# Attention with forget gates and a feed-forward network on one core: a tile of turned blocks per pair, split writes, product with v at the end of its slot, one tile of rounded q

## The chip, the cores and the metric

One core of a Trainium2 chip runs the whole program. The metric is the device time of one execution in microseconds. Engine names: PE is TensorE, DVE is VectorE, ACT is ScalarE, POOL is GpSimd, SP is the engine that issues the DMAs.

## The reference

64 heads (8 batches of 8 heads) of causal attention with 576 tokens and 64 columns per head, whose scores get a decay from the running sum of the logarithms of f. The heads of a batch are joined to 512 columns, and a layer norm with a two-layer network and a residual follows.

```python
scores = scale * q @ k.T                      # scale = 1/8, per batch and head
cum = np.cumsum(np.log(np.clip(f, 1e-4, 1.0)), axis=-1)
scores = np.where(causal, -1e9, scores + cum[:, :, :, None] - cum[:, :, None, :])
attn = softmax(scores)                        # sum + 1e-9 in the denominator
x = (attn @ v) -> (8, 576, 512)
xn = (x - mean) / sqrt(var + 1e-6) * g_ln
out = x + np.maximum(xn @ w_ch1, 0) @ w_ch2   # 512 -> 2048 -> 512
```

All is float32. The weights reach the device as 64-bit floats.

## The kernel before

Products that must keep float32 accuracy are made from rounded parts: a number is split into a high part (rounded, type fp32r) and a low part (the rest), and TensorE multiplies high by high, high by low and low by high.

The attention is cut in 256 slots: for each of 64 heads the row blocks t = 1 to 4 (128 queries each, with 192, 320, 448 and 576 keys; a block t=0 of 64 queries is done along with t=1). Heads 0 to 15 are "full": their products are in plain float32, and p is turned by TensorE. Heads 16 to 63 take another way, and most of the change concerns them:

- Q: the scores (qk_mm), two products for each piece of a row block. The first reads the high parts `hi`, the second reads `xq` (a copy of the rounded q beside two rows of ones) and `kl` (the low part of k beside the gates' sums).
- S: VectorE adds the mask and finds the row's extreme (softmax_a, L425). e: ScalarE's exponential with the row sum (L436). B: VectorE adds 1e-9 and inverts (L441, L442), and POOL scales p (L443).
- T: in the next slot VectorE turns p in blocks of 32 by 32 into the tile `pb` (turn, L461 and L463). The blocks are put in their final order by way of DRAM: `write` stores `pb` to `pd` (L471), and two slots after t=2 or t=4 V reads `pd` back into `pt` (L482, four DMAs). Blocks t=0, 1, 2 make pair 2, blocks t=3, 4 make pair 4.
- H and G: four slots after t=2 or t=4 ScalarE rounds `pt` into `ph` (L498 the rows and columns needed first, L502 the rest). l: VectorE writes the low part of the first columns (L506). o: POOL writes the low part of the rest (L513).
- A: five slots after, TensorE multiplies with v (av_unit, L606): high parts first, then low parts. F: ScalarE copies half of the result (L647). a: VectorE adds the other half into `xs` (L658), and every second head stores `xs` to DRAM (L660).

The feed-forward network works on 18 chunks of 256 tokens with 16 steps each. One step goes into each slot from slot 35 on, as soon as the heads of a batch are done; the steps that are left follow after the last slot. M is a step's first product (mm1, L691 to L693), r its Relu on ScalarE (L699), m its low part on VectorE (L704), N the second product of the step before (mm2, L713 to L715), R fetches and splits the next chunk's x (L674, L676) and turns rows back (chunk_rows), b copies these (L754) and takes their mean and variance.

Other letters: k rounds the next head's k and q and makes their low parts (t=1 and t=3), x copies the rounded q into `xq` (L353), P rounds v (L362), D loads raw q and k and v, W, w, f, g and s decode the weights during the first heads, L makes reciprocal roots.

The order of work on every engine is written by hand. For each slot the letters of one string are gone through from left to right, and each emits its instructions; each engine takes its own in that order. The string in force depends on the slot number:

```python
ORDERS = [
    (0, "WwQsSthAeMrgFBmlLNPaRf"),
    (37, "WwkQSTstAMhPeHlgNFGrxfmBoVDLRba"),
    (66, "kQSTAHeVGFtlahBoMPrxmNbRLD"),
]
```

PSUM is handed out by `bank`, six banks in turn for scores, products, first layers and turned rows; a bank is reused when its reader six allocations before is done.

Of the kernel before, what the change touches and what calls it, by code (L numbers as in the profile page):

```python
# [8 lines left out]
F32 = mybir.dt.float32  # L9
# [8 lines left out]
P = 128  # L18
# [40 lines left out]
def attn_moe(ctx: ExitStack, tc: tile.TileContext, qk, v, f, g, w1, w2, out):  # L59
# [26 lines left out]
    def busy(n):  # L86
# [6 lines left out]
    mask = const.tile([P, S], F32, tag="mask", name="mask")  # L93
    nc.gpsimd.memset(mask, 0.0)
    nc.gpsimd.affine_select(
        out=mask[:, S - P :], in_=mask[:, S - P :], pattern=[[-1, P]], base=0,
# [207 lines left out]
    def new_xq(name, dt):  # L304
        xq = work.tile([66, S], dt, tag="xq", bufs=2, name=name)
        nc.gpsimd.memset(xq[64:66, :].bitcast(F32), 1.0)
        return xq

    def load(n):
        h = Head()  # L310
        h.n, h.full = n, n < NFULL
        if h.full:
            h.kl = work.tile([66, S], F32, tag="kl", bufs=2, name=f"kl{n}")
            if len(xfs) < 2:
                xfs.append(new_xq(f"xf{n}", F32))
# [36 lines left out]
    def queries_copy(h):  # L352
        nc.scalar.copy(out=h.xq[0:64, :], in_=h.hi[0:64, 0, :].bitcast(F32))  # L353
# [36 lines left out]
    corners, padded, turned = [], {}, []  # L390
# [16 lines left out]
    def row_tile(h, t):  # L407
        nm = f"p{h.n}_{t}"
        if h.full and (4 * h.n + t - 1) % 3 == 0:
            if "late" in pools:  # L410
                return pools["late"].tile([P, 4 * 9 * 32], F32, tag="pb", bufs=1, name=nm)[:, 0:S]
            return wpool.tile([P, S], F32, tag="p", bufs=1, name=nm)
        return work.tile([P, S], F32, tag="p", bufs=2, name=nm)

    def softmax_a(h, t):
        q0, m, w = QT[t]
        nm = f"{h.n}_{t}"
        if t == 0:
            pt = corner(h.n)
        else:  # L420
            pt = row_tile(h, t)
        st = work.tile([P, 4], F32, tag="st", bufs=6, name=f"st{nm}")
        off = S - P - (w - m)
        for i, (a, z, sp) in enumerate(h.s[t]):
            nc.vector.tensor_tensor_reduce(  # L425
                out=pt[:m, a:z], in0=sp, in1=mask[:m, off + a : off + z], scale=-SCALE,
                scalar=3.0e38 if i == 0 else st[:m, 0:1], op0=ALU.add, op1=ALU.min, accum_out=st[:m, i : i + 1],
            )
        h.p = getattr(h, "p", {})
        h.p[t] = (pt, st)  # L430
# [16 lines left out]
    SLOTS = {0: (0, 0), 1: (1, 3), 2: (2, 4), 3: (0, 2), 4: (1, 5)}  # L447
# [5 lines left out]
    def turn(h, t):  # L453
        if not turned:
            turned.append(pools["late"].tile([P, 4 * 9 * 32], F32, tag="pb", bufs=1, name="pb"))
            nc.gpsimd.memset(turned[0], 0.0)
        pt, out_ = h.p[t][0], blocks(turned[0], t)
        first, rest = SLOTS[t]
        m = QT[t][1]
        rows = slice(64, P) if t == 0 else slice(0, P)  # L460
        nc.vector.transpose(out_[rows, 0:2, first, :], pt[:m, 0:64].rearrange("p (b i) -> p b i", i=32))  # L461
        if t > 0:
            nc.vector.transpose(  # L463
                out_[:, :, rest : rest + t, :].rearrange("p b k i -> p k b i"),
                pt[:, 64 : 64 + P * t].rearrange("p (k b i) -> p k b i", b=4, i=32),
            )

    def write(h, t):
        w = (6 if t == 2 else 9) * 32
        pd = dram.tile([P, 4 * w], F32, tag=f"pd{t}", bufs=2, name=f"pd{t}_{h.n}")  # L470
        nc.sync.dma_start(out=pd, in_=turned[0][:, : 4 * w])  # L471
        h.pd = getattr(h, "pd", {})
        h.pd[t] = pd

    def read(h, t):
        w, z = (6 * 32, 3 * 32) if t == 2 else (9 * 32, 2 * 32)
        tag = "pt1" if t == 2 else "pt2"
        pt = pools["late"].tile([P, 4 * w], F32R, tag=tag, bufs=1, name=f"{tag}_{h.n}")
        src = h.pd[t].rearrange("(a j) (b r) -> b j a r", a=4, b=4)
        for b in range(4):  # L480
            r = z if b > 1 else 0
            nc.sync.dma_start(  # L482
                out=pt[32 * b : 32 * b + 32, :].bitcast(F32).rearrange("j (a r) -> j a r", a=4)[:, :, r:],
                in_=src[b][:, :, r:],
            )
        h.pt = getattr(h, "pt", {})
        h.pt[t] = pt

    def parts_of(h, t):
        z = 3 if t == 2 else 2  # L490
        return z, blocks(h.pt[t], t), blocks(h.ph[t], t)

    def high_first(h, t):
        tag, w = ("ph1", 768) if t == 2 else ("ph2", 9 * P)
        h.ph = getattr(h, "ph", {})
        h.ph[t] = work.tile([P, w], F32R, tag=tag, bufs=1, name=f"{tag}_{h.n}")
        z, pt, ph = parts_of(h, t)
        nc.scalar.copy(out=ph[0:64, :, 0:z, :], in_=pt[0:64, :, 0:z, :].bitcast(F32))  # L498

    def high_rest(h, t):  # L500
        z, pt, ph = parts_of(h, t)
        nc.scalar.copy(out=ph[:, :, z:, :], in_=pt[:, :, z:, :].bitcast(F32))  # L502

    def low_first(h, t):
        z, pt, ph = parts_of(h, t)
        nc.vector.tensor_tensor(  # L506
            out=ph[64:128, :, 0:z, :], in0=pt[0:64, :, 0:z, :].bitcast(F32), in1=ph[0:64, :, 0:z, :].bitcast(F32),
            op=ALU.subtract,
        )

    def low_rest(h, t):
        z, pt, ph = parts_of(h, t)
        nc.gpsimd.tensor_tensor(  # L513
            out=pt[:, :, z:, :], in0=pt[:, :, z:, :].bitcast(F32), in1=ph[:, :, z:, :].bitcast(F32), op=ALU.subtract
        )
# [54 lines left out]
    def av_unit(h, t):  # L570
# [26 lines left out]
        z, low, high = parts_of(h, t)  # L597

        def acc(c0, c1, k, r, first=False):
            n = (c1 - c0) // P  # L600

            def view(x):
                return x[:, :, r : r + 3 * n - 2 : 3, :] if t == 4 and 1 <= k <= 3 else x[:, :, r : r + n, :]
# [7 lines left out]
            one(po[:, c0:c1], vv[:, k].rearrange("p a d -> p (a d)"), high, first)  # L611
# [4 lines left out]
        if t == 2:  # L616
            acc(0, 384, 0, 0, True)
            acc(128, 384, 1, 3)
            acc(256, 384, 2, 5)
            h.o = (po[:, 64:384], S1, 0)  # L620
        else:
            acc(0, 256, 0, 0, True)
            for k in range(1, 4):
                acc(0, 256, k, 1 + k)
# [26 lines left out]
    def finish_add(h):  # L651
# [210 lines left out]
    slots += [None] * (DONE + 1)  # L862
# [15 lines left out]
    for u, slot in enumerate(slots):  # L878
# [18 lines left out]
        def piece(c):  # L897
# [16 lines left out]
            elif c == "T" and past is not None:  # L914
                for i in [1, 0] if past[1] == 1 else [past[1]]:
                    turn(hd[past[0]], i)
                if past[1] in (2, 4):
                    write(hd[past[0]], past[1])
            elif c == "V" and due_read is not None:
                read(hd[due_read[0]], due_read[1])  # L920
            elif c == "H" and late is not None:
                high_first(hd[late[0]], late[1])
            elif c == "G" and late is not None:
                high_rest(hd[late[0]], late[1])
            elif c == "l" and late is not None:
                low_first(hd[late[0]], late[1])
            elif c == "k":
                two = before(2)
                if two is not None and two[1] == 4 and not hd[two[0]].full:
                    values_low(hd[two[0]])  # L930
# [3 lines left out]
            elif c == "x" and slot is not None and n + 1 >= NFULL and n + 1 < B * H and t == 3:  # L934
# [11 lines left out]
            elif c == "e" and slot is not None:  # L946
                for i in tiles(h, t):
                    softmax_e(h, i)
            elif c in FILL:
# [5 lines left out]
            elif c == "F" and av is not None:  # L955
                finish(av)
            elif c == "a" and av is not None:
                finish_add(av)
# [50 lines left out]
        def prep():  # L1009

            if before(1) is not None and before(1)[1] == 4 and not hd[before(1)[0]].full:
                values_high(hd[before(1)[0]])
# [56 lines left out]
```

## Time and profile before

| what | value |
|---|---|
| median of 3 runs | 1288.72 us (1286.53 to 1291.04) |
| the profiled execution | 1285.22 us, its span 1283.2 us |
| mean granted clock of TensorE | 0.987 |
| PE, DVE, ACT, POOL busy | 90%, 60%, 50%, 46% |
| DMA | 186.91 MB, 165169 packets |

The span is the time from the first to the last instruction that the profile holds. Busy shares are means over stages: slots of full heads (to about 283 us, with the weights decoded beside them), slots of the other heads (to about 1053 us), and the feed-forward steps that are left. "Idle before" a group of instructions is time in which its engine had nothing to run, with what ended it. PEld are weight loads, which run beside the products.

### The profile page before, as it was taken

Reading aid. Unit: us, or ns where it says so; the run is one execution under the profiler, and the core shown is the slowest. Engines: PE = TensorE matmul, PEld = TensorE weight load, DVE = VectorE, ACT = ScalarE, POOL = GpSimd, SP = SyncE. Lnnn points to the kernel's source line nnn. Section 1 sums busy time; section 2 is a strip of 40 time slices with the busy share of each in tenths; the row PEclk is TensorE's granted clock in tenths of the full one; section 3 lists DMA queues with packets and bytes.
Section 4 is the critical chain, followed back from the end, with each engine's and each line's share of the span. In section 5 each row is a group of like instructions: output and inputs, shape, how many; then the busy total and the mean of one; then the engine's idle time right before and its main releaser. Section 6 shows DMA issues by size and latency. Waiting matters only on the chain. (4 is left out here: it accounts for less than half of the span.)

```text
span 1283.2 us, 24610 instructions
## 1 busy us (share of the span) xinstructions
PE 1159.3 (90%) x7648; PEld 1025.9 (80%) x7648; DVE 770.7 (60%) x2706; ACT 646.2 (50%) x1744; POOL 594.3 (46%) x870
## 2 busy tenths in 40 slices
PE   8889999888988888988888988889888889999998
PEld 6657888778887787878787878788787879999997
DVE  6777774576757576666667676766666672222222
ACT  6886665455555555545555555555455542111111
POOL 3454454465556565555655565655555541000000
PEclk9999999999999999999999999999999999999999
DMA  6555532656656555647565656556565642110100
GB/s 182 161 146 159 159 83 66 187 165 184 185 169 178 161 172 186 195 153 203 174 182 175 200 166 179 157 186 180 170 189 175 187 149 60 45 38 18 50 25 25
DMA packets 165169, 186.91 MB, mean 146 GB/s; under 512 B 45488, under 2 KB 131504, under 8 KB 165040
## 3 DMA queue, kind: packets, MB, share of 16 engines
q1 hardware_dynamic: 165040, 185.35, 48.5%
q8 instruction: 61, 1.00, 0.3%
q14 instruction: 68, 0.56, 0.2%
HBM read 118.93 MB, written 66.36 MB: 144 GB/s over the span
## 5 line engine op out<-in xcount | busy, mean ns | idle before, releaser
L443 POOL TENSOR_SCALAR p<-p,st 64x64 f32<-64x64 f32 (+4 forms) x320 | 169.6, 535 | 434.6 <-DVE st L442 196.7
L691 PE MATMUL h<-x,w1h 128*128 128x256 f32 x1152 | 336.0, 292 | 0.4 <-DVE st L425 0.4
L692 PE MATMUL h<-x,w1h 128*128 128x256 f32 x1152 | 328.8, 285 | 0.0
L693 PE MATMUL h<-x,w1l 128*128 128x256 f32 x1152 | 328.8, 285 | 0.0
L436 ACT ACTIVATE p<-p,st 64x64 f32<-64x64 f32 (+4 forms) x320 | 179.1, 560 | 264.4 <-DVE st L425 244.9
L704 DVE SCALAR_TENSOR_TENSOR hh<-h,hh 128x256 fp32r<-128x256 f32 x288 | 121.7, 422 | 229.1 <-ACT hh L699 227.5
L713 PE MATMUL acc<-w2h,hh 128*128 128x512 f32 x576 | 230.7, 401 | 0.0
L714 PE MATMUL acc<-w2l,hh 128*128 128x512 f32 x576 | 229.8, 399 | 0.0
L699 ACT ACTIVATE hh<-h 128x256 fp32r<-128x256 f32 x288 | 109.6, 380 | 237.7 <-PE h L693 236.1
L715 PE MATMUL acc<-w2h,hh 128*128 128x512 f32 x576 | 227.0, 394 | 0.0
L691 PEld LDWEIGHTS h<-x,w1h 128*128 128x128 f32 x1152 | 221.6, 192 | 5.5 <-issue 0.9
L692 PEld LDWEIGHTS h<-x,w1h 128*128 128x128 f32 x1152 | 222.9, 193 | 2.5
L693 PEld LDWEIGHTS h<-x,w1l 128*128 128x128 f32 x1152 | 223.1, 194 | 0.0
L425 DVE CUSTOM_DVE_ANT_0 p<-s,mask 64x64 f32<-64x64 f32 (+4 forms) x320 | 130.5, 422 | 82.4 <-PE s L385 76.6
L513 POOL TENSOR_TENSOR pt<-pt,ph 128x384 fp32r<-128x384 f32 x96 | 149.5, 1558 | 6.1 <-ACT ph L502 6.1
L606 PE MATMUL o<-pt,vv 128*64 128x256 f32 (+1 forms) x288 | 48.9, 278 | 101.4 <-POOL pt L513 97.8
L715 PEld LDWEIGHTS acc<-w2h,hh 128*128 128x128 f32 x576 | 109.7, 190 | 25.3
L713 PEld LDWEIGHTS acc<-w2h,hh 128*128 128x128 f32 x576 | 111.3, 193 | 14.5 <-ACT ph_full L568 0.2
L606 PEld LDWEIGHTS o<-pt,vv 128*64 128x64 f32 x288 | 29.6, 135 | 115.4 <-POOL pt L513 115.4
L714 PEld LDWEIGHTS acc<-w2l,hh 128*128 128x128 f32 x576 | 111.0, 193 | 12.0
L658 DVE TENSOR_TENSOR xs<-o,ot 64x320 f32<-64x320 f32 x96 | 43.2, 450 | 125.8 <-ACT ot L647 125.8
L776 POOL TENSOR_SCALAR sv<-sv 128x2 f32<-128x2 f32 x18 | 3.9, 215 | 188.9 <-DVE sv L760 187.7
(87 smaller groups left out, 2013.9 us busy)
## 6 DMA issues: line engine op xcount, KB each, us to landing
raw<-in_qk_dram SPq DMA_DIRECT2D x96, 288.0 KB
pd<-pb SPq DMA_DIRECT2D x48, 576.0 KB
pd<-pb SPq DMA_DIRECT2D x48, 384.0 KB
wr<-in_w_dram SPq DMA_DIRECT2D x32, 512.0 KB
pt<-pd SPq DMA_DIRECT2D x96, 144.0 KB
pt<-pd SPq DMA_DIRECT2D x96, 112.0 KB
vr<-in_v_dram SPq DMA_DIRECT2D x64, 160.0 KB
out_dram<-xt SPq DMA_DIRECT2D x36, 256.0 KB
```

The lines of the kernel that those rows point to most:

```text
L425: nc.vector.tensor_tensor_reduce(out=pt[:m, a:z], in0=sp, in1=mask[:m, off + a : off + z], scale=-SCALE, scalar=3.0e38 if i == 0 else st[: ...
L436: nc.scalar.activation(pt[:m, :w], pt[:m, :w], AF.Exp, bias=st[:m, i : i + 1], scale=-1.0, accum_out=st[:m, 2:3])
L443: nc.gpsimd.tensor_scalar(out=pt[:m, :w], in0=pt[:m, :w], scalar1=st[:m, 3:4], scalar2=1.0, op0=ALU.mult, op1=ALU.mult)
L513: nc.gpsimd.tensor_tensor(out=pt[:, :, z:, :], in0=pt[:, :, z:, :].bitcast(F32), in1=ph[:, :, z:, :].bitcast(F32), op=ALU.subtract)
L691: mm(ph, w1h[:, k, fs], c.x[k][:, 0, :], start=(k == 0), stop=False)
L692: mm(ph, w1h[:, k, fs], c.x[k][:, 1, :], start=False, stop=False)
L693: mm(ph, w1l[:, k, fs], c.x[k][:, 0, :], start=False, stop=(k == KT - 1))
L699: nc.scalar.activation(h[:, 0, :], c.ph, AF.Relu)
L704: nc.vector.scalar_tensor_tensor(out=h[:, 1, :], in0=ph, scalar=0.0, in1=h[:, 0, :].bitcast(F32), op0=ALU.max, op1=ALU.subtract)
L713: mm(c.acc[i], h[:, 0, ts_], w2h[:, j, :], start=(j == 0), stop=False)
L714: mm(c.acc[i], h[:, 0, ts_], w2l[:, j, :], start=False, stop=False)
L715: mm(c.acc[i], h[:, 1, ts_], w2h[:, j, :], start=False, stop=(j == FT - 1))
```

## The change

For heads 16 to 63:

- Each pair has a tile of turned blocks of its own (`pb2`, `pb4`), and the blocks lie in another order (`SLOTS`). Each t from 1 to 4 writes its own columns (`WRITES`; t=0 goes with t=1) by itself, at the end of its turn's slot (letter d), so a head has four writes for two.
- The reads take all rows and columns.
- The exponential and the softmax's second part follow directly on the turn; the cast of `pt` is one instruction and comes behind them, and the two low parts behind it. POOL's low part is two instructions.
- The product with v stands behind both feed-forward products of its slot. The copy of its result, the sum and the store come one slot later (`fin`), the store at that slot's end (letter X).
- `xq` is one tile for two, and its copy moves from t=3 to t=4. The rounding of v and its low part come one slot later.
- The mask tile has 128 columns fewer, and the feed-forward's limit and the empty slots at the end move by one slot.

```diff
 ORDERS = [
-    (0, "WwQsSthAeMrgFBmlLNPaRf"),
-    (37, "WwkQSTstAMhPeHlgNFGrxfmBoVDLRba"),
-    (66, "kQSTAHeVGFtlahBoMPrxmNbRLD"),
+    (0, "WwQsSthAeMrgFBmlLNPaXRf"),
+    (37, "WwkQSTstAMhPeHlgNFrxfmBoDLRbaXdV"),
+    (67, "kQSTeBHloFaMNAPxrmbRLdDVX"),
 ]
...
-        if len(xqs) < 2:
-            xqs.append(new_xq(f"xq{len(xqs)}", F32R))
-        h.xq = xqs[(n - NFULL) % 2]
...
     def queries_copy(h):
+        if not xqs:
+            xqs.append(new_xq("xq", F32R, work))
+        h.xq = xqs[0]
         nc.scalar.copy(out=h.xq[0:64, :], in_=h.hi[0:64, 0, :].bitcast(F32))
...
-    SLOTS = {0: (0, 0), 1: (1, 3), 2: (2, 4), 3: (0, 2), 4: (1, 5)}
+    SLOTS = {0: (1, 0), 1: (2, 0), 2: (3, 4), 3: (3, 0), 4: (4, 5)}
+    WRITES = {1: (0, 3), 2: (3, 6), 3: (0, 4), 4: (4, 9)}
...
     def write(h, t):
+        i = t + t % 2
+        w = (6 if i == 2 else 9) * 32
+        h.pd = getattr(h, "pd", {})
+        if t % 2 == 1:
+            h.pd[i] = dram.tile([P, 4 * w], F32, tag=f"pd{i}", bufs=2, name=f"pd{i}_{h.n}")
+        r0, r1 = WRITES[t]
+        a, b = (x.rearrange("p (b r) -> p b r", b=4)[:, :, 32 * r0 : 32 * r1] for x in (h.pd[i], turned[i]))
+        nc.sync.dma_start(out=a, in_=b)
...
+    FIRSTS = {2: (1, 4), 4: (3, 5)}
...
-    def high_first(h, t):
+    def high(h, t):
...
+        nc.scalar.copy(out=h.ph[t], in_=h.pt[t].bitcast(F32))
...
     def low_rest(h, t):
+        pt, ph = parts_of(h, t)
+        w = 6 if t == 2 else 9
+        for r in (slice(0, FIRSTS[t][0]), slice(FIRSTS[t][1], w)):
+            nc.gpsimd.tensor_tensor(
+                out=pt[:, :, r, :], in0=pt[:, :, r, :].bitcast(F32), in1=ph[:, :, r, :].bitcast(F32), op=ALU.subtract
+            )
...
         if j == 1:
-            nc.sync.dma_start(out=(xd1 if g1 else xd2)[b][P * pr : P * pr + P, :], in_=xs)
+            h.store = ((xd1 if g1 else xd2)[b][P * pr : P * pr + P, :], xs)
...
+        fin = av if av is not None and av.full else None
+        if before(DONE + 1) is not None and before(DONE + 1)[1] in (2, 4) and not hd[before(DONE + 1)[0]].full:
+            fin = hd[before(DONE + 1)[0]]
...
+            elif c == "d" and past is not None:
+                write(hd[past[0]], past[1])
...
-            elif c == "x" and slot is not None and n + 1 >= NFULL and n + 1 < B * H and t == 3:
+            elif c == "x" and slot is not None and n + 1 >= NFULL and n + 1 < B * H and t == 4:
                 queries_copy(hd[n + 1])
...
-                moe.limit = min(NCHUNK, max(0, min(u - LAG - 1, max(4 * NFULL, u - DONE))) // (4 * H) * S // C)
+                moe.limit = min(NCHUNK, max(0, min(u - LAG - 1, max(4 * NFULL, u - DONE - 1))) // (4 * H) * S // C)
```

More of the change, by code (lines that the diff above doesn't have):

```diff
@@ L92, in attn_moe @@
     busy(WARM[1])
-    mask = const.tile([P, S], F32, tag="mask", name="mask")
+    mask = const.tile([P, S - P], F32, tag="mask", name="mask")
     nc.gpsimd.memset(mask, 0.0)
     nc.gpsimd.affine_select(
-        out=mask[:, S - P :], in_=mask[:, S - P :], pattern=[[-1, P]], base=0,
+        out=mask[:, S - 2 * P :], in_=mask[:, S - 2 * P :], pattern=[[-1, P]], base=0,
         channel_multiplier=1, compare_op=ALU.is_ge, fill=NEG,
@@ L302, in attn_moe, with new_xq @@
     xqs, xfs = [], []
-    def new_xq(name, dt):
-        xq = work.tile([66, S], dt, tag="xq", bufs=2, name=name)
+    def new_xq(name, dt, pool):
+        xq = pool.tile([66, S], dt, tag="xq", bufs=1, name=name)
         nc.gpsimd.memset(xq[64:66, :].bitcast(F32), 1.0)
@@ L388, in qk_mm @@
             h.s[t].append((a, z, sp))
-    corners, padded, turned = [], {}, []
+    corners, padded, turned = [], {}, {}
     def padded_keys(tag, width, zeros):
@@ L410, in row_tile @@
             if "late" in pools:
-                return pools["late"].tile([P, 4 * 9 * 32], F32, tag="pb", bufs=1, name=nm)[:, 0:S]
+                return pools["late"].tile([P, 4 * 9 * 32], F32, tag="pb4", bufs=1, name=nm)[:, 0:S]
             return wpool.tile([P, S], F32, tag="p", bufs=1, name=nm)
@@ L422, in softmax_a @@
         st = work.tile([P, 4], F32, tag="st", bufs=6, name=f"st{nm}")
-        off = S - P - (w - m)
+        off = S - 2 * P - (w - m)
         for i, (a, z, sp) in enumerate(h.s[t]):
             nc.vector.tensor_tensor_reduce(
-                out=pt[:m, a:z], in0=sp, in1=mask[:m, off + a : off + z], scale=-SCALE,
+                out=pt[:m, a:z], in0=sp, in1=mask[:m, max(0, off + a) : max(0, off + a) + z - a], scale=-SCALE,
                 scalar=3.0e38 if i == 0 else st[:m, 0:1], op0=ALU.add, op1=ALU.min, accum_out=st[:m, i : i + 1],
@@ L454, in turn @@
         if not turned:
-            turned.append(pools["late"].tile([P, 4 * 9 * 32], F32, tag="pb", bufs=1, name="pb"))
-            nc.gpsimd.memset(turned[0], 0.0)
-        pt, out_ = h.p[t][0], blocks(turned[0], t)
+            for i, w in ((2, 6), (4, 9)):
+                turned[i] = pools["late"].tile([P, 4 * w * 32], F32, tag=f"pb{i}", bufs=1, name=f"pb{i}")
+                nc.gpsimd.memset(turned[i], 0.0)
+        pt, out_ = h.p[t][0], blocks(turned[t + t % 2 if t > 0 else 2], t)
         first, rest = SLOTS[t]
@@ L468, in write, with read @@
     def write(h, t):
-        w = (6 if t == 2 else 9) * 32
[L470 to L476, printed above, removed]
+        i = t + t % 2
[6 more added lines that the diff above has]
+        nc.sync.dma_start(out=a, in_=b)
+    def read(h, t):
+        w = (6 if t == 2 else 9) * 32
         tag = "pt1" if t == 2 else "pt2"
@@ L480, in read @@
         for b in range(4):
-            r = z if b > 1 else 0
             nc.sync.dma_start(
-                out=pt[32 * b : 32 * b + 32, :].bitcast(F32).rearrange("j (a r) -> j a r", a=4)[:, :, r:],
-                in_=src[b][:, :, r:],
+                out=pt[32 * b : 32 * b + 32, :].bitcast(F32).rearrange("j (a r) -> j a r", a=4), in_=src[b]
             )
@@ L487, in read @@
         h.pt[t] = pt
+    FIRSTS = {2: (1, 4), 4: (3, 5)}
     def parts_of(h, t):
-        z = 3 if t == 2 else 2
-        return z, blocks(h.pt[t], t), blocks(h.ph[t], t)
-    def high_first(h, t):
+        return blocks(h.pt[t], t), blocks(h.ph[t], t)
+    def high(h, t):
         tag, w = ("ph1", 768) if t == 2 else ("ph2", 9 * P)
@@ L496, in high_first @@
         h.ph[t] = work.tile([P, w], F32R, tag=tag, bufs=1, name=f"{tag}_{h.n}")
[L497 to L502, printed above, removed]
+        nc.scalar.copy(out=h.ph[t], in_=h.pt[t].bitcast(F32))
     def low_first(h, t):
-        z, pt, ph = parts_of(h, t)
+        pt, ph = parts_of(h, t)
+        r = slice(*FIRSTS[t])
         nc.vector.tensor_tensor(
-            out=ph[64:128, :, 0:z, :], in0=pt[0:64, :, 0:z, :].bitcast(F32), in1=ph[0:64, :, 0:z, :].bitcast(F32),
+            out=ph[64:128, :, r, :], in0=pt[0:64, :, r, :].bitcast(F32), in1=ph[0:64, :, r, :].bitcast(F32),
             op=ALU.subtract,
@@ L511, in low_rest @@
     def low_rest(h, t):
[L512 to L515, printed above, removed]
+        pt, ph = parts_of(h, t)
+        w = 6 if t == 2 else 9
[3 more added lines that the diff above has]
+            )
     def tr(out_, in_):
@@ L596, in av_unit, with acc @@
         vv = h.vv
-        z, low, high = parts_of(h, t)
-        def acc(c0, c1, k, r, first=False):
+        low, high_ = parts_of(h, t)
+        def acc(c0, c1, k, r, step=1, first=False):
             n = (c1 - c0) // P
             def view(x):
-                return x[:, :, r : r + 3 * n - 2 : 3, :] if t == 4 and 1 <= k <= 3 else x[:, :, r : r + n, :]
+                return x[:, :, r : r + step * (n - 1) + 1 : step, :]
             def one(o, st, x, first):
@@ L609, in one @@
                 )
-            one(po[:, c0:c1], vv[:, k].rearrange("p a d -> p (a d)"), high, first)
+            one(po[:, c0:c1], vv[:, k].rearrange("p a d -> p (a d)"), high_, first)
             if k > 0:
@@ L616, in av_unit @@
         if t == 2:
-            acc(0, 384, 0, 0, True)
-            acc(128, 384, 1, 3)
+            acc(0, 384, 0, 1, first=True)
+            acc(128, 384, 1, 0, 4)
             acc(256, 384, 2, 5)
@@ L621, in av_unit @@
         else:
-            acc(0, 256, 0, 0, True)
+            acc(0, 256, 0, 3, first=True)
             for k in range(1, 4):
-                acc(0, 256, k, 1 + k)
+                acc(0, 256, k, k - 1, 5)
             acc(128, 256, 4, 8)
@@ L659, in finish_add, with store @@
         if j == 1:
-            nc.sync.dma_start(out=(xd1 if g1 else xd2)[b][P * pr : P * pr + P, :], in_=xs)
+            h.store = ((xd1 if g1 else xd2)[b][P * pr : P * pr + P, :], xs)
+    def store(h):
+        if getattr(h, "store", None) is not None:
+            out_, xs = h.store
+            nc.sync.dma_start(out=out_, in_=xs)
+            h.store = None
     class Chunk:
@@ L861, in attn_moe @@
     nu = len(slots)
-    slots += [None] * (DONE + 1)
+    slots += [None] * (DONE + 2)
     hd = {}
@@ L921, in piece @@
             elif c == "H" and late is not None:
-                high_first(hd[late[0]], late[1])
-            elif c == "G" and late is not None:
-                high_rest(hd[late[0]], late[1])
+                high(hd[late[0]], late[1])
             elif c == "l" and late is not None:
@@ L927, in piece @@
             elif c == "k":
-                two = before(2)
-                if two is not None and two[1] == 4 and not hd[two[0]].full:
-                    values_low(hd[two[0]])
+                three = before(3)
+                if three is not None and three[1] == 4 and not hd[three[0]].full:
+                    values_low(hd[three[0]])
                 if slot is not None and n + 1 >= NFULL and n + 1 < B * H and t in (1, 3):
@@ L948, in piece @@
                     softmax_e(h, i)
+            elif c == "X" and fin is not None:
+                store(fin)
             elif c in FILL:
@@ L954, in piece @@
                     busy(WARM[2])
[L955 to L958, printed above, removed]
+            elif c == "F" and fin is not None:
+                finish(fin)
+            elif c == "a" and fin is not None:
+                finish_add(fin)
             elif c == "r" and want:
@@ L1009, in prep @@
         def prep():
-            if before(1) is not None and before(1)[1] == 4 and not hd[before(1)[0]].full:
-                values_high(hd[before(1)[0]])
+            if before(2) is not None and before(2)[1] == 4 and not hd[before(2)[0]].full:
+                values_high(hd[before(2)[0]])
             if slot is not None:
```

4 lines of the change are left out of this document (1 added, 3 removed).

## The prediction

> **What bounds the kernel now.** I read the stages first (one row per stretch: busy time of each engine, TensorE clock, DMA share), then the list of waits, then the instructions in order of time over one head, then the groups by shape.
>
> ```profile
> PE 1159.3 (90%) x7648; PEld 1025.9 (80%) x7648; DVE 770.7 (60%) x2706; ACT 646.2 (50%) x1744; POOL 594.3 (46%) x870
> ...
> 283.00:1053.00 770.00, 677.02 (x4395) 611.92 (x4394) 519.16 (x1867) 415.20 (x1075) 440.07 (x592) 0.98 0.59 178
> 1053.00:1283.00 230.00, 224.34 (x1450) 203.19 (x1448) 58.62 (x138) 43.94 (x113) 20.57 (x75) 1.00 0.13 39
> ...
> PEld o L606 <- POOL pt L513: 115.4, 94, 2.7
> PE o L606 <- POOL pt L513: 97.8, 64, 2.5
> ACT p L436 <- DVE st L425: 244.9, 180, 3.0
> ```
>
> TensorE bounds it: 90% busy, at a granted clock of 0.98 to 1.00. No other engine is near full in the middle stretch (DVE 519 of 770 us). After 1053 us only feed-forward steps are left, TensorE is nearly solid there, and their number is fixed, so nothing in that stretch changes. The change lives in the middle stretch, where heads 16 to 63 run. There TensorE stands still mostly for one thing: the low-part products with v (L606) wait for POOL's subtraction (L513). Weight loads lose 115.4 us to it, matmuls 97.8. The ends of matmuls are modelled, so I count the weight loads' number, 115.4, as what TensorE loses, with 97.8 as the lower end.
>
> Now one stretch of one head in the order of time (start, duration, engine, line). A head has four slots, t = 1 to 4; the rows begin with t=4 and go over into t=1 of the next head.
>
> ```profile
> 700.84 0.30 PE L384 MATMUL s<-hi 128*128 128x288 f32 x1
> 701.31 0.46 DVE L425 CUSTOM_DVE_ANT_0 p<-s,mask 128x288 f32<-128x288 f32 x1 [0.68 <-PE s L385]
> 701.38 0.28 PE L691 MATMUL h<-x,w1h 128*128 128x256 f32 x1
> 702.54 0.78 ACT L436 ACTIVATE p<-p,st 128x576 f32<-128x576 f32 x1 [1.65 <-DVE st L425]
> 703.32 0.92 ACT L502 CAST ph<-pt 128x896 fp32r<-128x896 f32 x1
> 704.06 0.75 POOL L443 TENSOR_SCALAR p<-p,st 128x576 f32<-128x576 f32 x1 [2.91 <-DMA pt<-pd]
> 704.15 0.37 ACT L699 ACTIVATE hh<-h 128x256 fp32r<-128x256 f32 x1
> 704.21 0.25 PE L384 MATMUL s<-hi 128*128 128x192 f32 x1
> 704.30 0.28 PE L385 MATMUL s<-kl,xq 66*128 66x192 f32 x1
> 704.54 0.75 PE L606 MATMUL o<-ph,vv 128*128 128x256 f32 x5
> 704.77 2.09 POOL L513 TENSOR_TENSOR pt<-pt,ph 128x896 fp32r<-128x896 f32 x1
> 706.91 0.62 PE L606 MATMUL o<-pt,vv 128*64 128x256 f32 x4 [1.63 <-POOL pt L513]
> ...
> 282.28 0.78 ACT L436 ACTIVATE p<-p,st 128x576 f32<-128x576 f32 x1 [1.08 <-DVE st L425]
> ...
> 1053.29 0.78 ACT L436 ACTIVATE p<-p,st 128x576 f32<-128x576 f32 x1 [2.21 <-DVE st L425]
> ```
>
> The reader sees the ring. In t=4 ScalarE casts the blocks (703.32), POOL scales p (704.06) and then subtracts (704.77 to 706.86), and TensorE, which reached the products at 704.54, stands from 705.29 to 706.91. The semaphore takes 0.05 us (706.86 to 706.91). The last two rows are the same exponential of heads 19 and 63 (count 64 of that shape in the groups): 771.0 us for 44 heads, 17.5 us a head.
>
> **The change, part by part.** I count all times from the start of t=4's scores (700.84 = 0).
>
> *Product with v at the slot's end, after both feed-forward products.* In t=1 of the next head TensorE now does the scores (0.24 us from 704.30 to 704.54), then the feed-forward step, 2.83 us (701.38 to 704.21 is one whole step), and only then the products. POOL's subtraction has to be done by then. It starts, as now, when p is scaled (704.06 + 0.75, 3.97) and is cut in two pieces:
>
> ```profile
> L513 POOL TENSOR_TENSOR pt<-pt,ph 128x896 fp32r<-128x896 f32 x48 | 100.5, 2093 | 5.5 <-ACT ph L502 5.5
> L513 POOL TENSOR_TENSOR pt<-pt,ph 128x384 fp32r<-128x384 f32 x48 | 49.1, 1022 | 0.5 <-ACT ph L502 0.5
> L502 ACT CAST ph<-pt 128x896 fp32r<-128x896 f32 x48 | 44.5, 926 | 0.0
> L502 ACT CAST ph<-pt 128x384 fp32r<-128x384 f32 x48 | 23.9, 497 | 0.0
> L647 ACT COPY ot<-o 64x320 f32<-64x320 f32 x48 | 20.3, 423 | 3.3 <-PE o L606 2.2
> L353 ACT CAST xq<-hi 64x576 fp32r<-64x576 f32 x48 | 31.8, 662 | 0.0
> L754 ACT COPY xt<-xp 128x512 f32<-128x512 f32 x36 | 20.8, 577 | 0.0
> L676 DVE TENSOR_TENSOR x<-xr,x 128x256 fp32r<-128x256 f32 x66 | 60.6, 938 | 3.5 <-ACT x L674 3.5
> ```
>
> The two POOL shapes give 2.09 ns a column (1071 ns for 512). Pair 4's pieces are 384 and 512 columns: 1.02 + 1.29 = 2.31, ended at 6.28. TensorE gets to the products at 7.6 at the earliest (worked out below), 1.4 us later. Pair 2 is cast in t=2 and multiplied at the end of t=3, with more room. So the whole wait goes: minus 115 us (minus 98 at least). The extra 0.22 us of POOL is hidden by those 1.4 us.
>
> *One tile of rounded q.* The copy (L353) moves from t=3 to t=4, because with one tile it may be written only when t=4's scores are done. This is what is late next. On ScalarE's queue t=4 now reads: exponential, cast of pair 4, copy of the output part, q copy, Relu. The exponential cannot start sooner, since it waits for VectorE's pass over the scores (idle 1.65 before 702.54). It starts at 1.70, and the next instruction at 2.48. The cast is now one piece of 1152 columns; the two cast shapes give 0.838 ns a column, so 926 + 256 x 0.838 = 1.14 us, and 1.05 until the next may start (instructions overlap by 0.09: 703.32 + 0.92 against 704.15). The output copy takes 0.42, 0.33 to the next. The q copy takes 0.66. Sum 2.48 + 1.05 + 0.33 + 0.66 = 4.52, with the semaphore 4.57. TensorE asks for it in the second score product of t=1 (L385, which reads xq), today at 704.30, 3.46. New stall: 1.11 us a head, for 47 heads plus 52 us. Its lower end is nothing, if TensorE were late there for other reasons. The upper end is 94 us, at 2 us a head, if VectorE starts t=4 late (a rival below). I take the row sum. Queued behind the stalled score product is the feed-forward step of t=1.
>
> *What the stall and the lost cover do to the feed-forward step.* Today the step of t=1 starts only after the products and their wait, at 707.38, 6.54. Now it starts at 4.57 + 0.24 = 4.81. Two things that were ready in time may not be. Once in a chunk (16 slots, four heads) two x parts are split in t=4 after the Relu part: VectorE is free for them near 5.35 and needs 2 x 0.94, done 7.2; the step's last quarter wants the second near 6.0. That is 1.2 us, 12 times, plus 14 (0 to 18). And once in a chunk the PSUM bank that the step takes was that of the turned rows, whose copy (L754) comes after q copy and Relu: 4.52 + 0.27 + 0.58 = 5.4 against 4.8, plus 7 (0 to 7).
>
> *Exponential, reciprocal and scaling ahead of casts.* The exponential gains nothing, since it waited for VectorE and not for its place. VectorE now stands at the small adds until the exponential is done, and behind them queue the low parts, the output sum, values and the Relu's low part. Whom that could hurt is t=4's pass over the scores:
>
> ```profile
> 716.75 0.42 DVE L704 SCALAR_TENSOR_TENSOR hh<-h,hh 128x256 fp32r<-128x256 f32 x1
> 718.00 0.46 DVE L425 CUSTOM_DVE_ANT_0 p<-s,mask 128x288 f32<-128x288 f32 x1 [0.82 <-PE s L385]
> ...
> L425 DVE CUSTOM_DVE_ANT_0 p<-s,mask 128x448 f32<-128x448 f32 x64 | 39.3, 615 | 15.4 <-PE s L385 13.3 <-PE s L382 2.1
> L506 DVE TENSOR_TENSOR ph<-pt,ph 64x384 fp32r<-64x384 f32 x48 | 24.5, 510 | 0.0
> L658 DVE TENSOR_TENSOR xs<-o,ot 64x256 f32<-64x256 f32 x48 | 20.0, 417 | 63.3 <-ACT ot L647 63.3
> L362 DVE CAST vv<-vr 128x320 fp32r<-128x320 f32 x48 | 22.0, 459 | 0.0
> ```
>
> Today VectorE is idle 0.82 us there. In the new order, by TensorE's rows alone, t=1's scores resume at 4.6, t=2 starts at 8.7 (4.81, the step's 2.83, some 1.0 of products), t=3 at 11.8 and the next t=4 at 15.5. t=2 is the full slot for VectorE. Its exponential ends near 10.3, the cast of 768 columns (0.82) at 11.1, the output copy at 11.4. Behind these VectorE does the low part (0.51), the output sum (0.42), the values (0.46) and the Relu part (0.42), and is done at 12.9, about 0.5 after t=3's scores are ready. Then follow 0.6 for t=3's scores, the exponential, the small adds and the Relu part, done at 15.2. t=4's scores are ready at 15.5 + 0.47 (701.31 against 700.84), so 0.8 us of room remain, and only the one head in four with an x split in t=2 loses about 0.1. With the drain after the last head I put plus 4 for this (0 to 24, at 0.5 us a head).
>
> *Writes and reads of the turned blocks.* Two writes a head become four, 0.34 us each on SP's queue (row below); 96 more issues are 33 us, spread over a queue that does nothing but issue and wait. The write goes from the turn to the slot's end, before the raw load and the reads, and it waits for the turn. The raw load behind it waits for POOL's key part anyway. The reads of pair 4 are issued near 10.7 (after t=2's write), and their cast comes at 15.5 + 2.48 = 18.0: 7.3 us.
>
> ```profile
> 706.16 0.34 SPq L471 DMA_DIRECT2D pd<-pb  x1
> ...
> 709.00 1.74 SPq L482 DMA_DIRECT2D pt<-pd  x4
> ...
> 717.18 0.41 ACT L498 CAST ph<-pt 64x256 fp32r<-64x256 f32 x1
> ...
> 726.68 0.38 SPq L325 DMA_DIRECT2D raw<-in_qk_dram  x1
> ...
> 730.85 0.67 ACT L350 CAST hi<-raw 128x576 fp32r<-128x576 f32 x1 [1.17 <-DMA raw<-in_qk_dram]
> ```
>
> Today the reads have 8.2 us (709.00 to 717.18) and the cast is never kept waiting. How long they really need is not shown. The nearest row is the raw load, 4.17 us from issue to a cast that waited for it; the last of four reads starts 1.3 us after the first, so I estimate 5.5 us, 1.8 less than there is. I take nothing for it; the upper end is a rival.
>
> *The rest.* Two blocks tiles in place of one take away a 3.5 us wait of VectorE, which is off the path. Mask, tile places and the later store: nothing, within 1 us. The feed-forward limit comes one slot later, and 230 us of steps are left over at the end as a store.
>
> **Sum.** 115 off; 52, 14, 7 and 4 on: minus 38 us. The profiled execution took 1285.2 us (span 1283.2), so 1247; the median of the runs shown stands 3.5 us above that execution, so 1250.
>
> **The rivals.** (1) *The row sum*, 1250; with each term between its ends 1232 to 1268.
> (2) *Cheaper*: the two feed-forward terms do not appear. Minus 115 + 52 = minus 63, 1226. For it: the rows show x parts ready early today. Against: they were covered by the very wait that goes.
> (3) *VectorE starts t=4 late*: then the ring of scores, exponential, cast, q copy is longer. Each 0.1 us costs 4.7; at 0.8 us late a head the gain is gone (1288). For it: three of four slots now hold VectorE behind the exponential. Against: 0.8 us of room worked out above.
> (4) *Late block reads, slower*: by the code, write pieces go from one run of 3072 or 4608 bytes per partition to four of 384 to 640 bytes, and the reads take all columns. If a read lands more than 7.3 us after its issue, ScalarE stands at the cast with the output copy, the q copy and so TensorE behind it, 47 us for each us. It decides against the change from 2.6 us over my estimate of 5.5 (0.8 x 47 = 38); at 4 us over it gives 1250 + 2.2 x 47 = 1353. For it:
>
> ```profile
> DMA packets 165169, 186.91 MB, mean 146 GB/s; under 512 B 45488, under 2 KB 131504, under 8 KB 165040
> ```
>
> Packets under 512 bytes exist today, and the chip's DMA share is 0.59 in this stretch. Against: no cast has ever waited for its blocks. [...]
> (5) *It does not do what it says*: the subtraction still ends last. That needs POOL 1.4 us later than worked out; little speaks for it, and it falls in (3) by its times.
>
> **How the numbers follow.** (1) 0.55; (2) 0.13; (3), with (5), 0.18, 1268 to 1292, of it 0.10 faster, 0.05 same, 0.03 slower; (4) 0.14, slower. A difference under 0.3%, 4 us, cannot be told from none. Faster 0.55 + 0.13 + 0.10 = 0.78, same 0.05, slower 0.03 + 0.14 = 0.17. The range 1224 to 1288 leaves out (4), the slow end of (3) and the tail of (2).
>
> **What would show it.** Right: L606's wait for POOL gone; in its place the score product of t=1 (the line of qk_mm that reads xq) waiting for ScalarE's q copy about 1.1 us in 47 places; a head's period near 16.7 us. The x and bank terms show as waits of the first feed-forward matmul. Wrong: the big cast waiting for the block reads (4), VectorE with no idle time before t=4's scores (3), or L606 still waiting (5).

## The result and the profile after

The changed kernel takes 1247.63 us (median of 4 runs, 1242.01 to 1248.68) against 1287.83 us for the kernel before in the same series: a ratio of 0.9675, with a 95% interval of 0.9641 to 0.9710. The forecast was 1250 us, faster. The profiled execution took 1248.68 us (span 1246.9), 36.5 less than that of before. One execution of `a_back` below, at 3840.2 us, is left out of its time and ratio; with it the median is 1301.2 us.

The page's busy times and the stages (busy time of each engine in the stretch, then TensorE's clock, DMA share, GB/s):

```profile
PE 1150.8 (92%) x7648; PEld 1017.4 (82%) x7648; DVE 759.5 (61%) x2706; ACT 641.0 (51%) x1648; POOL 633.9 (51%) x966
...
283.00:1019.00 736.00, 665.43 (x4395) 600.76 (x4394) 510.58 (x1868) 409.98 (x987) 476.54 (x680) 0.99 0.71 195
1019.00:1247.00 228.00, 223.79 (x1445) 202.60 (x1443) 58.20 (x136) 44.45 (x112) 21.77 (x78) 1.00 0.15 43
```

The gain lies in the middle stretch: the same 4395 products take 736 us for 770. The stretch behind it is within some 2 us of what it was. The list of waits shows what TensorE stands for now:

```profile
PEld s L385 <- ACT xq L353: 68.7, 46, 2.4
PE s L385 <- ACT xq L353: 55.3, 46, 2.1
PEld o L608 <- POOL vv L365: 20.3, 12, 1.7
PE o L608 <- POOL vv L365: 15.2, 12, 1.3
PEld h L700 <- DVE x L684: 7.5, 12, 0.6
PE h L700 <- DVE x L684: 5.0, 12, 0.4
```

The product with v (now L608) no longer waits for POOL's low part of p: that row, 115.4 us before, is gone. In its place 46 score products wait for the q copy, 12 products with v for the low part of v, and 12 feed-forward products for the split x. One ring in the order of time:

```profile
649.42 0.37 PE L384 MATMUL s<-hi 128*128 128x288 f32 x1
651.20 0.78 ACT L436 ACTIVATE p<-p,st 128x576 f32<-128x576 f32 x1 [1.83 <-DVE st L425]
651.97 1.14 ACT L501 CAST ph<-pt 128x1152 fp32r<-128x1152 f32 x1
652.85 0.25 PE L384 MATMUL s<-hi 128*128 128x192 f32 x1
653.13 0.42 ACT L649 COPY ot<-o 64x320 f32<-64x320 f32 x1
653.33 2.42 POOL L515 TENSOR_TENSOR pt<-pt,ph 128x384 fp32r<-128x384 f32 x2
653.46 0.67 ACT L353 CAST xq<-hi 64x576 fp32r<-64x576 f32 x1
654.18 0.36 PE L385 MATMUL s<-kl,xq 66*128 66x192 f32 x1 [1.08 <-ACT xq L353]
657.37 0.70 PE L608 MATMUL o<-ph,vv 128*128 128x256 f32 x5
...
281.25 0.78 ACT L436 ACTIVATE p<-p,st 128x576 f32<-128x576 f32 x1 [2.46 <-DVE st L425]
...
1018.75 0.78 ACT L436 ACTIVATE p<-p,st 128x576 f32<-128x576 f32 x1 [2.45 <-DVE st L425]
```

Counted from t=4's scores (649.42 = 0): exponential at 1.78, cast at 2.55, output copy at 3.71, q copy at 4.04, score product at 4.76 (forecast 1.70, 2.48, 3.53, 3.86, 4.57). POOL is done at 6.33 (forecast 6.28), and TensorE comes to the products at 7.95 (7.6). A score product that came 0.09 after the one ahead of it now comes 1.33 after it. The last two rows, heads 19 and 63 again, give 737.5 us for 44 heads, 16.8 us a head for 17.5; the forecast said near 16.7.

### The profile page after: what moved, and what is told of

Same layout as the page of the kernel before. It is cut to its first block, busy times and chain, and to the rows that moved or that the text cites. A ratio compares the mean times of both kernels' runs of the same rounds, so it can differ in the third digit from the quotient of the medians.

```text
span 1246.9 us, 24808 instructions
## 1 busy us (share of the span) xinstructions
PE 1150.8 (92%) x7648; PEld 1017.4 (82%) x7648; DVE 759.5 (61%) x2706; ACT 641.0 (51%) x1648; POOL 633.9 (51%) x966
## 2 busy tenths in 40 slices
DMA packets 252724, 194.80 MB, mean 156 GB/s; under 512 B 83888, under 2 KB 231344, under 8 KB 252592
## 4 chain that ended last, share of the span: by engine, by line
PE 57%; ACT 14%; DVE 11%; DMA 7%; issue 7%; POOL 2%; SPq 1%; ACTq 0%; DVEq 0%; POOLq 0%
PE h L699 7%; PE h L700 7%; PE h L701 7%; PE acc L721 7%; PE acc L722 7%; PE acc L723 7%; PE o L608 5%; ACT ph L501 5%; ACT p L436 3%; DVE p L425 3%; PE s L385 2%; DMA pd<-pb 2%; ACT xq L353 2%; ACT ot L649 2%; PE s L384 2%
## 5 line engine op out<-in xcount | busy, mean ns | idle before, releaser
L712 DVE SCALAR_TENSOR_TENSOR hh<-h,hh 128x256 fp32r<-128x256 f32 x288 | 121.4, 421 | 208.8 <-ACT hh L707 208.7
L700 PEld LDWEIGHTS h<-x,w1h 128*128 128x128 f32 x1152 | 219.9, 191 | 10.6 <-DVE x L684 7.5
L699 PEld LDWEIGHTS h<-x,w1h 128*128 128x128 f32 x1152 | 219.3, 190 | 6.6 <-issue 0.9
L701 PEld LDWEIGHTS h<-x,w1l 128*128 128x128 f32 x1152 | 220.4, 191 | 0.0
L515 POOL TENSOR_TENSOR pt<-pt,ph 128x128 fp32r<-128x128 f32 x192 | 186.1, 987 | 6.9 <-ACT ph L501 6.9
L385 PE MATMUL s<-kl,xq 66*128 66x288 f32 (+4 forms) x288 | 82.8, 309 | 55.3 <-ACT xq L353 55.3
L385 PEld LDWEIGHTS s<-kl,xq 66*128 66x128 f32 (+1 forms) x288 | 52.3, 181 | 71.1 <-ACT xq L353 68.7
L501 ACT CAST ph<-pt 128x768 fp32r<-128x768 f32 x96 | 94.0, 979 | 5.0 <-DMA pt<-pd 4.5
```

Source lines behind the costliest of these rows:

```text
L385: mm(sp, xq, kl, start=False, stop=True)
L501: nc.scalar.copy(out=h.ph[t], in_=h.pt[t].bitcast(F32))
L515: nc.gpsimd.tensor_tensor(out=pt[:, :, r, :], in0=pt[:, :, r, :].bitcast(F32), in1=ph[:, :, r, :].bitcast(F32), op=ALU.subtract)
L699: mm(ph, w1h[:, k, fs], c.x[k][:, 0, :], start=(k == 0), stop=False)
L700: mm(ph, w1h[:, k, fs], c.x[k][:, 1, :], start=False, stop=False)
L701: mm(ph, w1l[:, k, fs], c.x[k][:, 0, :], start=False, stop=(k == KT - 1))
```

## The experiments

All ratios are to the kernel before, run on the same chip in the same series; "changed" is the changed kernel's 1247.6 us. The kernel before had medians of 1284.0 to 1287.8 us in these series, so a difference between two kernels of different series is good to some 4 us. My theory was the ring: the moved product frees TensorE of POOL's wait, and the q copy at the end of ScalarE's queue in t=4 takes half of that back. The first rival was that the new order on ScalarE, VectorE and POOL brought the gain.

**The product's place alone, added to the kernel before** (`only_a_end`).

```diff
-    (66, "kQSTAHeVGFtlahBoMPrxmNbRLD"),
+    (67, "kQSTHeVGFtlahBoMPrxmNAbRLD"),
+        # F and a work on the result of the slot before (fin); values_high, values_low one slot later
```

> The kernel before with one part of the change alone: the product with v goes behind the feed-forward products, with what this needs (result copy, sum and store one slot later, the values' rounding one slot later, the feed-forward limit one slot later). Two xq tiles with the copy in t=3, one tile of turned blocks, two writes, casts ahead of the exponential stay. Theory: the 115 us wait for POOL's low part goes, and the q copy makes no new wait; the waits for the low part of v (about 20 us) and for the split x (about 10) come as in the changed kernel, and POOL's low part, which starts later behind the casts, leaves little room. 1205 to 1230, so faster than the whole change (1248). Rival (the new order behind the exponential is needed for the gain, because scaling comes too late otherwise): the wait for POOL's low part stays in part, 1255 to 1280.

1221.2 us, ratio 0.9511 (0.9481 to 0.9540). One part of the change alone brings 63 us; the whole change brings 40. Its weight loads wait for:

```profile
PEld o L606 <- POOL vv L365: 31.2, 35, 2.7
PEld o L606 <- POOL pt L513: 24.2, 35, 1.1
```

Of 115.4 us of waiting for POOL's low part 24.2 stay; the theory puts that down to the casts, which still stand ahead of the exponential and let POOL start later. So TensorE's place brings the gain, and the rest of the change as made costs some 21 (by the ratios) to 26 us (by the times).

**The product put back in the changed kernel** (`a_back`, and once more for its waits, `a_back2`).

```diff
-    (67, "kQSTeBHloFaMNAPxrmbRLdDVX"),
+    (67, "kQSTAeBHloFaMNPxrmbRLdDVX"),
+        # values_high, values_low one slot earlier, as before the change
```

> The changed kernel with the product with v put back ahead of the feed-forward products (behind the turn), and the rounding of v and its low part back one slot earlier, as before the change. All else is as changed. Theory: the wait for POOL's low part comes back, shorter than before because the product now starts after the q-copy stall: about 1.0 us a head for pair 4 and 0.3 for pair 2, plus 50 to 65 us, less the 15 to 20 us of waits for the low part of v: about 1285 (1270 to 1300). Rival (the new order on ScalarE, VectorE and POOL brought the gain, not TensorE's place): within 10 us of 1248.

> The same edit as a_back (product with v ahead of the feed-forward products again, values one slot earlier, the rest as changed), for its waits; its time was 1301 where 1285 was expected. Theory: the wait for POOL's low part is back beside the q copy's: 45 to 65 us for POOL at the weight loads, 60 to 75 for the q copy, and what is missing to 1301 is TensorE's clock, granted at 0.97 or less in the middle stretch because both stalls fall into one slot. Rival (a longer POOL chain alone): over 85 us of waits for POOL, clock 0.98 or more.

1300.0 and 1299.0 us, ratio 1.0107 (1.0041 to 1.0173) for the second: 1% slower than before, 51 us slower than changed, and at the upper end of the 1270 to 1300 expected. In the second:

```profile
PEld s L385 <- ACT xq L353: 66.2, 46, 1.8
PEld o L608 <- POOL pt L515: 49.8, 94, 1.4
PEld o L608 <- POOL p L443: 13.8, 12, 1.2
```

Both waits have the expected size. The clock was granted at 0.982 of full speed, not at the 0.97 that the theory expected; I estimate its loss as span times missing share, 1296.4 x 0.018 = 23 us against 1246.9 x 0.010 = 12 in the changed kernel. Together the rows of the weight loads and the clock explain some 44 of the 51 us (50 and 14 on, 20 and 8 off for v and x, 3 off at the q copy, 11 for the clock).

**The q copy twice** (`x_twice`).

```diff
         nc.scalar.copy(out=h.xq[0:64, :], in_=h.hi[0:64, 0, :].bitcast(F32))
+        nc.scalar.copy(out=h.xq[0:64, :], in_=h.hi[0:64, 0, :].bitcast(F32))
```

> The copy of the rounded q into xq is issued twice in a row; nothing else changes. Theory (ring: scores of t=4, exponential, big cast, output copy, q copy, second score product of t=1): the copy is on the path in 46 heads, so each extra 0.57 to 0.66 us of ScalarE goes straight into the time: plus 26 to 31 us, about 1276, and the wait of the score product for the copy grows from 55 to about 83 us. Rival (the wait is slack that other work would fill anyway): within 5 us of 1248.

1301.3 us, ratio 1.0108 (1.0044 to 1.0172): 54 us more than changed, about twice what was expected. The weight loads' wait grows from 68.7 to 101.2 us, 0.7 a head, as the theory has it (one line further down in this kernel):

```profile
PEld s L386 <- ACT xq L354: 101.2, 47, 3.1
```

What the theory had left out is the clock, 0.965 for 0.990. Stretches of 3.41 us show it (columns as in the stages above):

```profile
412.54:415.95 3.41, 1.51 (x13) 1.22 (x11) 1.73 (x5) 3.31 (x8) 3.33 (x5) 1.00 0.91 252
415.95:419.36 3.41, 3.41 (x12) 2.90 (x12) 2.42 (x13) 1.59 (x6) 2.20 (x4) 0.50 0.04 12
419.36:422.78 3.42, 3.42 (x27) 3.30 (x26) 2.74 (x10) 1.08 (x3) 0.00 (x0) 1.00 0.59 203
```

A stretch in which TensorE is busy 1.51 of 3.41 us is followed by one at half the clock, in which it does 12 products where the stretch behind it does 27, in part of other shapes. By its mean clock this kernel loses an estimated 1302.7 x 0.035 = 46 us, 33 more than the changed kernel. With the 32 us of longer waits that is 65, more than the 56 between the two profiled executions, so the two overlap in part.

**The q copy early** (`x_early`).

```diff
-    (67, "kQSTeBHloFaMNAPxrmbRLdDVX"),
+    (67, "kQxSTeBHloFaMNAPrmbRLdDVX"),
```

> The q copy stands right behind the scores in the queue, ahead of the exponential, where ScalarE is idle today; one tile as before. Theory: the score product no longer waits for it (55 us and 69 us at the weight loads go), but the feed-forward product behind it is then asked for near 3.7 us of t=4 and needs a PSUM bank that VectorE frees with the output sum near 4.5, so a new wait of about 0.85 us a head takes most of it back: minus 20 to 30 us, 1218 to 1228. Rival (the copy is the only thing late there): minus 55 to 65, about 1187.

1204.8 us, ratio 0.9345 (0.9275 to 0.9414), 43 us faster than changed. The copy fits into ScalarE's idle time ahead of the exponential (at 663.74), still with one tile:

```profile
662.55 0.67 ACT L353 CAST xq<-hi 64x576 fp32r<-64x576 f32 x1 [1.43 <-PE s L385]
```

Its list of weight loads' waits begins, in heads 16 to 63, with:

```profile
PEld o L608 <- POOL vv L365: 21.5, 12, 2.1
PEld h L700 <- DVE x L684: 17.0, 12, 1.6
```

Both sides missed. The score product's wait is gone, and the PSUM bank that I expected to take its place does not appear among the waits. Why not 60 us: the wait for the split x rose from 7.5 to 17.0, and the clock lost an estimated 1206.2 x 0.022 = 27 us for 12.

**The root steps later** (`l_later`).

```diff
-    (67, "kQSTeBHloFaMNAPxrmbRLdDVX"),
+    (67, "kQSTeBHloFaMNAPxrmLbRdDVX"),
```

> The reciprocal-root steps on POOL stand ahead of the rows' statistics in the order, so they are taken up one slot later and no longer sit in POOL's queue ahead of the low part of v. Theory: the 12 waits of the product with v for the low part of v (20 us at the weight loads, 15 at the products) go: minus 13 to 20 us, about 1231. Rival (these waits are covered by the q-copy ring and only move): within 5 us of 1248.

1248.2 us, ratio 0.9697 (0.9636 to 0.9757): no gain. The wait for v's low part is gone, and others grew:

```profile
PEld s L385 <- ACT xq L353: 73.7, 46, 3.1
PEld acc L723 <- DVE hh L712: 12.7, 18, 0.9
```

20.3 off, 5.0 and 12.7 on. VectorE's end of a chunk now waits for the root steps, a row that the changed kernel does not have:

```profile
DVE xt L798 <- POOL rs L792: 23.9, 12, 2.1
```

The Relu's low part (L712) stands behind it in VectorE's order; that the 12.7 us come from there is argued, not shown.

**Both repairs** (`x_v_early`): the q copy early, and v's low part on POOL directly behind its rounding, ahead of the root steps.

```diff
                 values_high(hd[before(2)[0]])
+                values_low(hd[before(2)[0]])
...
-                three = before(3)
-                if three is not None and three[1] == 4 and not hd[three[0]].full:
-                    values_low(hd[three[0]])
```

> The changed kernel with the q copy right behind the scores (as in the run before, 1204.8) and the low part of v taken directly behind its rounding in t=2, ahead of the reciprocal-root steps on POOL. Theory: the 12 waits for the low part of v (20 us at the weight loads, 15 at the products) go and nothing takes their place, because the root steps keep their slot: 1185 to 1192. Rival (as with the later root steps, the wait only moves): 1200 to 1210.

1183.9 us, ratio 0.9232 (0.9195 to 0.9270), 1 us below the expected range, and the best of all versions. In heads 16 to 63 its weight loads no longer wait for v; what is left is nearly all for the split x:

```profile
PEld h L700 <- DVE x L684: 24.3, 24, 1.2
PEld h L699 <- ACT x L682: 5.3, 12, 0.6
```

**The same in the kernel before with the product at the end** (`only_a_v_early`).

> The kernel before with the product at the slot's end alone (1221) and the low part of v taken directly behind its rounding in t=2. Theory: its waits for the low part of v (28 us at the weight loads) go, those for POOL's low part of p (24 us) stay, since the casts still stand ahead of the exponential and so delay POOL: 1195 to 1205, which leaves some 12 to 20 us to the version of the changed kernel with both repairs (1184). Rival (the rest of the change is worth nothing): 1180 to 1190.

1207.4 us, ratio 0.9387 (0.9339 to 0.9435), 2 us above the expected range.

```profile
PEld o L606 <- POOL pt L513: 23.5, 35, 1.1
PEld o L606 <- POOL vv L365: 12.7, 23, 1.3
```

The wait for POOL's low part of p stays as it was, and that for v goes only in part. So once its two new waits are repaired, the change without the product's place (scaling ahead of the casts, and what goes with it) is worth some 20 us by the ratios, 23 by the times: 1183.9 for 1207.4. Which part of it does so was not tried.

**A further repair that failed** (`x_v_split`): `room = KT if left == 0 else 3 if left == 1 else 2`, on top of both.

> The version with both repairs (1184) with one more: the third x part of a chunk is split one slot earlier (t=3), so that t=4 splits one part and not two before the next chunk's first product. Theory: the wait of the first product for the split x (24 us at the weight loads, 24 times) falls to a few us, and VectorE's extra 0.94 us in t=3 is covered, because the q copy no longer hangs on t=4's exponential: 1164 to 1174. Rival (VectorE late in t=3 delays the block casts and the Relu parts, and a new wait takes the place): 1180 to 1190.

1204.2 us, ratio 0.9366 (0.9301 to 0.9430): 20 us slower than without it.

```profile
PEld h L700 <- DVE x L684: 18.8, 12, 1.6
PEld h L699 <- ACT x L682: 15.8, 12, 1.7
```

The waits did not go. They are fewer and longer, 34.6 us for 29.6, and the granted clock is 0.982 for 0.992, an estimated 1201.0 x 0.018 = 22 us lost for 9. Both sides missed: the rival was right that waits stay, but the time is 14 us above its range, and by this estimate the clock accounts for 13. Why the parts come later was not tried.

**One q tile in the kernel before** (`only_one_xq`): one tile, its copy in t=4.

> The kernel before with one xq tile and its copy in t=4, nothing else. Theory: the score product of t=1 then waits for the copy about 1 us, but TensorE stands 1.6 us behind it anyway for POOL's low part, whose chain the copy does not touch: no change, within 6 us of 1287, with the wait moved from the product with v to the score product. Rival (the copy's wait always costs): plus 45 to 55, about 1335.

1291.5 us, ratio 1.0052 (1.0029 to 1.0075): 7.5 us slower than before in the same series, where no change within 6 us was forecast, and far from the rival's 45 to 55.

```profile
PEld o L606 <- POOL pt L513: 75.4, 94, 2.1
PEld s L385 <- ACT xq L353: 45.6, 46, 1.8
```

115.4 us of one wait became 75.4 and 45.6 of two: the copy's stall is nearly free as long as POOL's wait stands behind it.

**Reads one slot later** (`read_late`): `READ, HIGH, DONE = 3, 4, 5`.

> The changed kernel with the turned blocks read back one slot later (three slots after t=2 and t=4 in place of two). Theory: the reads now land 3.3 us (pair 4) and 3.5 us (pair 2) before their casts by the packets' times; one slot of 3.5 to 4.5 us later makes the casts wait about 1 to 4 us each, which for pair 4 goes fully into the ring: plus 50 to 200 us, with the big cast waiting for the DMA. Rival (much more room, the reads are far from late): within 10 us of 1248.

1613.3 us, ratio 1.2561 (1.2517 to 1.2606): 366 us slower than changed, nearly twice the top of what I gave.

```profile
ACT ph L501 <- DMA pt<-pd: 288.1, 87, 6.0
PEld s L385 <- ACT xq L353: 254.7, 46, 7.1
```

Nearly all casts of both pairs wait, 3.3 us each, and the q copy behind the casts hands it on to TensorE: its wait grew from 68.7 to 254.7 us. The clock, 0.889, loses an estimated 1611.5 x 0.111 = 179 us, 166 more than in the changed kernel; the expectation had no clock in it.

**One write a pair** (`one_write`): `pd` is written once, with t=2 and t=4.

> The changed kernel with one write for each pair's whole tile at the end of the turn's slot of t=2 and t=4, in place of one for each t. Theory: the reads have about 3 us of room, so writes in smaller pieces cost nothing and bring nothing: within 6 us of 1248. Rival (pieces below 512 bytes or the two further issues load the DMA queues): 8 us or more faster.

1247.6 us, ratio 0.9706 (0.9666 to 0.9747), the same as changed within the intervals. DMA packets under 512 bytes fall from 83888 to 33200 with it, by the pages of the two kernels. So the pieces of 384 to 640 bytes and the two more writes a head show no cost here.

## Why the prediction was right, step by step

*The wait that goes*: right. The row of 115.4 us is gone, and the product's place does it, shown from both sides: added alone, with what it needs, it brings 63 us, taken out it costs 51.

*The ring through the q copy*: right in place and order, slightly short in size. Forecast 1.11 us in 47 heads, 52 us; by starts it is 1.33 - 0.09 = 1.24 in 46, 57 us (55.3 and 68.7 by the two rows). The step that ran over is the big cast: 1.14 us as worked out, but the output copy began 1.16 after it (651.97 to 653.13), where I had taken off 0.09 for overlap.

*The feed-forward terms*: too high. The split x took 5.0 to 7.5 us where I put 14, and the PSUM bank that was to cost 7 is not among the waits.

*VectorE late*, 4 us: no wait of TensorE shows it by itself. Its pass over t=4's scores starts 0.54 after them in this ring (0.47 before), and the exponential 0.08 later than forecast; at 46 heads that is about 4 us, which the ring's 57 already hold:

```profile
649.96 0.46 DVE L425 CUSTOM_DVE_ANT_0 p<-s,mask 128x288 f32<-128x288 f32 x1
```

*What was left out*: 15 to 20 us for the low part of v. I followed its move on VectorE, not on POOL's queue. Before, it was taken up at the start of t=2; now it is taken up at the start of t=3, and t=2's end has put the root steps ahead of it, once a chunk:

```profile
664.02 0.21 POOL L784 TENSOR_SCALAR sv<-sv 128x2 f32<-128x2 f32 x1 [1.06 <-DVE sv L768]
...
665.42 0.19 POOL L792 TENSOR_TENSOR rs<-rs 128x2 f32<-128x2 f32 x1
665.57 0.87 POOL L365 TENSOR_TENSOR vv<-vr,vv 128x320 fp32r<-128x320 f32 x1
...
666.50 0.62 PE L608 MATMUL o<-ph,vv 128*128 128x384 f32 x3 [1.26 <-POOL vv L365]
```

POOL waits for VectorE's variance, does six small steps to 665.61, and only then the low part, to 666.44; TensorE starts 0.06 later.

*The sum*: better than its parts, and in part luck. What came is 57 + 15 + 5 = 77 us (the first by starts, the others by the matmul rows), as forecast, with two terms too high and one missing. And the sum takes what goes by the weight loads (115.4) and what comes by the matmuls' times. With the same rows on both sides it is 115.4 - 68.7 - 20.3 - 7.5 = 18.9 by the weight loads, or 97.8 - 55.3 - 15.2 - 5.0 = 22.3 by the matmuls; measured were 36.5. The stages agree with the second: TensorE's idle time in the middle stretch fell from 770.00 - 677.02 = 93.0 to 736.00 - 665.43 = 70.6 us, by 22.4. The other 11.6 of that stretch's 34 us are busy time: the same 4395 products took less. TensorE was at half its clock in seven stretches of 3.41 us there before (the first at 356.41), in three after (469.77, 538.04 and 606.30), which I estimate at 12 and 5 us of lost work. So some 7 are the clock's, for which the forecast had no term. Where the last 5 come from stays open; as the ends of matmuls are modelled, the split into idle and busy is rough.

*The row sum's span*: 1232 to 1268 does not follow from "each term between its ends"; the ends given would make it 1173 to 1333.

*The reads' room*: right. The casts wait 4.5 us for the blocks in all, in the page's groups:

```profile
L501 ACT CAST ph<-pt 128x768 fp32r<-128x768 f32 x96 | 94.0, 979 | 5.0 <-DMA pt<-pd 4.5
```

Rival (4) did not come, but one slot less turns it on, so its mechanism stands. Its price of 47 us for each us was low: casts 3.3 us late would cost 155 by it, and 366 were measured, with the clock's 166 among them. The smaller write pieces show no effect on this time: the kernel with one write a pair, with 33200 packets under 512 bytes for 83888, takes the same 1247.6 us.

## What to carry to other kernels

Ask of each instruction that is moved what stands ahead of it on every queue that it or its inputs pass, in the slot where that queue is fullest: the one cost missed here was on the queue that seemed to have time. When a long wait is taken off the bound engine, list what used to be ready "in time" only because of it; a copy that was nearly free under the old wait cost 57 us without it, and moving that copy into idle time ahead of the exponential, without a second tile, brought 43 us back. Price what goes and what comes by the same rows of the profile, or the sum can be right by luck. And try a change's parts one by one: one part alone was faster than the whole.

## What the runs showed of the hardware

In the traces of the kernels before and after, TensorE's clock falls to 0.50 for one stretch of 3.41 us at a time: nine times before (seven in the middle stretch) and once more from 1281.41 to the end, and seven times after (three there). The stretch ahead of each ran at 1.00, with TensorE busy 0.99 to 2.40 of 3.41 us, so it was partly idle. It need not be idle throughout: in the rows of `x_twice` it was busy 1.51 of 3.41 us. The same two steps recur there at 450.08 and 487.63, 34.13 and 37.55 us on, ten and eleven such stretches later, so the stretches seem to lie on a fixed grid:

```profile
446.67:450.08 3.41, 1.51 (x10) 1.09 (x9) 1.39 (x5) 3.31 (x6) 2.87 (x3) 1.00 0.78 222
450.08:453.49 3.41, 3.41 (x15) 3.21 (x15) 2.30 (x13) 1.98 (x7) 2.33 (x4) 0.50 0.77 235
...
487.63:491.04 3.41, 3.41 (x12) 2.92 (x12) 2.42 (x13) 1.60 (x6) 2.21 (x4) 0.50 0.03 7
```

The busy share alone does not decide it. In the kernel before, of two stretches busy 1.78 and 1.79 of 3.41 us, that from 353.00 is followed by one at 0.50 and that from 721.64 by one at 1.00. What decides stays open.

I estimate that a stretch at half the clock loses up to 1.7 us of work, half of 3.41. In the changed kernel the waits for the q copy, 1.5 us each (68.7 in 46), went with a clock of 0.990; with the copy doubled they were 2.2 us each (101.2 in 47), and the clock was 0.965. That is part of why doubling the copy cost 54 us where its waits grew by 32, and it goes with the failure of the last repair, whose waits were fewer and longer.
